# Two linear-attention blocks on one core: the place of A's head selection on VectorE, and which of B's weight buffers holds which sum of pk

## The chip, the core and the metric

The kernel runs on one core of a Trainium2 chip. The core has a matrix engine (TensorE, "PE" in the profile, with its weight loads "PEld"), a vector engine (VectorE, "DVE"), an activation engine (ScalarE, "ACT"), GpSimd ("POOL") and a sync engine (SyncE, "SP") whose queue issues nearly all of the DMAs here. Each engine works through its own instructions in order and waits on semaphores for the others. The metric is the device time of one execution in microseconds; of several runs the median is given.

## The reference

Two blocks A and B with weights of their own read the same x (2048 rows of 640), and a gate mixes their outputs:

```python
qkv = ((x @ wqkv).reshape(B, S, 3, H, Dh)).transpose(2, 0, 3, 1, 4)      # H = 32, Dh = 20
q, k, v = qkv[0], qkv[1], qkv[2]
phi = lambda t: jnp.where(t > 0, t + 1, jnp.exp(t)) + 1e-6
pq, pk = phi(q), phi(k)
kv = jnp.einsum("bhsd,bhse->bhde", pk, v)
z = jnp.einsum("bhsd->bhd", pk)
num = jnp.einsum("bhqd,bhde->bhqe", pq, kv)
den = jnp.einsum("bhqd,bhd->bhq", pq, z)[..., None] + 1e-6
block = (num / den).transpose(0, 2, 1, 3).reshape(B, S, D) @ wo
...
g = sigmoid((x * gate_w).sum(-1, keepdims=True))
return g * block_A + (1 - g) * block_B
```

All tensors are bf16.

## The kernel before

**What is computed.** v is never formed. Because v = x wv, the product of pk and v is (x^T pk)^T wv, so each block first makes G = x^T pk, a 640 x 640 matrix kept transposed in halves in `GT`, and then multiplies by wv and keeps only the diagonal blocks of 20 x 20 per head (`kvt_mm`, `kvt_mask` for B, `kv_a` for A). These blocks times wo give one 640 x 640 matrix M per block (`m_a` for A, `m_unit` and `m_half` for B), and the output is pq M, where pq has been multiplied by gate / den beforehand (`scale`, line 551).

**Order of the work.** Both blocks use the same stages: k (`k_chunk`, line 207) and q (`q_unit`, line 256) with phi on ScalarE and VectorE; then `g_all` (line 665) with G; then wv, wo and the output. A's k and q come first, then A's G; then B's k, with A's small products between them; then B's q and B's G; then the output of both blocks together, by seven products of halves in place of eight (class `Pair`). From line 699 on the order of all engines' instructions is the order in which the code issues them (`tc.manual_schedule`), so the place of a line in the code is its place in its engine's queue.

**G in `g_all`.** The fifth column block of x is done by `g_pass`: 16 row tiles i, two matmuls each (`g_mm`, line 297). The other four column blocks are done by `g_strassen`, seven products of halves (`g_prod`, line 324, 16 matmuls each) in place of eight. Its operands are the halves themselves, four differences of x made once (`SX[1]` to `SX[4]`, by `x_sum`, in block A only) and four sums of pk made for each block (`TK[b][1]` to `TK[b][4]`, by `k_sum`). All of these sums are VectorE's (line 501). The seven products in order: x11 b11, SX[2] TK[2], x12 b21, SX[3] TK[3], SX[1] TK[1], x22 TK[4], SX[4] b22.

**z and the normalisation.** Between the row tiles of `g_pass`, ahead of i = 6, PE sums pk over all rows from TK[3] and TK[4] (`z_rows`); ScalarE and VectorE copy the result (`zr`). Ahead of i = 14 `z_pass` issues five small matmuls (line 402), which bring zr into columns, and a VectorE instruction (line 406) that selects the heads by a mask and writes `zsel`. zsel is the weight operand of the denominators (`rec_pass`, lines 171 and 491 to 496), which come on PE directly behind the last row tile. For block A the VectorE work issued ahead of i = 6 is: the copy of zr, the first x difference `x_sum(1)`, the two gate instructions (line 183), and the second x difference `x_sum(2)`.

**Weight buffers.** wk, wv, wq and wo have one buffer each, which serves A's weight first and B's later. B's wk and wq are loaded while A runs. B's wv and wo come last: while B's q and G are computed, their two buffers (and wk's) hold B's sums of pk. Before: T1 is in wv's buffer, T4 in wk's, T2 and T3 share wo's. A buffer is free for its load when its last reader on PE is done. The loads are issued from SP: `load_wo(1)` in the code behind the fourth product (line 359, issue at line 656), `load_w(1, "v")` behind the fifth (line 369, issue at line 641). Nothing else is on SP's queue between the load of M[0] (line 462) and the stores of the output (line 582).

**Behind G in B.** PE's first matmuls behind the seventh product are `kvt_mm(1, kv, 0)` (line 416), which reads wvB and the low half of GT; then come the first product of the output, `kvt_mm(1, kv, 1)`, another product of the output, and `m_unit` (line 476), the first reader of woB. VectorE has in that place the last two GT adds (line 377), the two masks (line 423) and the first of the sums of M.

Of the kernel before, what the change touches and what calls it, by code (L numbers as in the profile page):

```python
# [8 lines left out]
P = 128  # L9
FP32 = mybir.dt.float32  # L10
BF16 = mybir.dt.bfloat16
# [10 lines left out]
HF = D // 2  # L22
# [11 lines left out]
def kernel(  # L34
# [11 lines left out]
    nc = tc.nc  # L46
# [42 lines left out]
    hc, ic = ST // 2, 2 * P  # L89
# [22 lines left out]
    wk = [None, None]  # L112
# [63 lines left out]
    def gate_pass():  # L176

        pt = ps("lg", 2)
        for h in range(2):
            by_group(pt[:, 1, h * RB:(h + 1) * RB], gwr, xT, h)  # L180
        for b in range(2):
            nc.scalar.activation(out=ge[b][:], in_=pt[:, 1, :], func=ACT.Exp, scale=(-1.0, 1.0)[b])
            nc.vector.tensor_scalar(ge[b][:], ge[b][:], 1.0, 1e30, op0=ALU.add, op1=ALU.min)
# [94 lines left out]
    def g_pass(b, c, slot):  # L278

        pt = ps(f"g{'AB'[b]}", slot)  # L280
        for i in range(ST):
            if i == 6:
                zt, zr = z_rows(b, 0)
                if b == 0:
                    x_sum(1)
                    gate_pass()
                    x_sum(2)
            if i == 14:
                zsel = z_pass(zt, zr)
            for hf in range(2):  # L290
                g_mm(c, i, hf, pt)
        for hf in range(2):
            nc.scalar.copy(out=GT[hf][:, c, :], in_=pt[:, hf, 0:HF])
        return zsel
# [7 lines left out]
    def x_sum(k):  # L302

        x11, x21 = [xn[:, 0:hc, n:n + ic] for n in (0, ic)]
        x12, x22 = [xn[:, hc:ST, n:n + ic] for n in (0, ic)]
        a, b, op = {
            1: (x21, x22, ALU.subtract), 2: (x11, SX[1], ALU.subtract),
            3: (x21, x11, ALU.subtract), 4: (x12, SX[2], ALU.subtract),
        }[k]
        add_rows(SX[k], a, b, op)  # L310
# [18 lines left out]
    def g_strassen(b, norm):  # L329

        x11, x12 = [xn[:, k:k + hc, 0:ic] for k in (0, hc)]
        x22 = xn[:, hc:ST, ic:2 * ic]
        b11 = pk[:, 0:hc, 0:HF]
        b21, b22 = [pk[:, hc:ST, n * HF:(n + 1) * HF] for n in range(2)]
        lo, hi = GT

        def temp(name):
            return work.tile([P, 2, HF], FP32, tag="osb", name=name, bufs=3)

        def add(dst, pt, sb):  # L340
            nc.vector.tensor_tensor(out=dst, in0=pt[:, :, 0:HF], in1=sb[:], op=ALU.add)

        even, odd = ps("gs0", 0), ps("gs1", 1)
        g_prod(even, x11, b11, True)
        p1 = temp("p1")
        nc.scalar.copy(out=p1[:], in_=even[:, :, 0:HF])
        g_prod(odd, SX[2], TK[b][2], True)
        u2 = temp("u2")
        add(u2[:], odd, p1)
        if b == 0:  # L350
            x_sum(3)
        norm()
        g_prod(even, x12, b21, False)
        nc.scalar.copy(out=lo[:, 0:2, :], in_=even[:, :, 0:HF])
        scale(b, 0)
        scale(b, 1)
        g_prod(odd, SX[3], TK[b][3], False)
        if b == 1:
            load_wo(1, nc.sync)
        u3 = temp("u3")  # L360
        add(u3[:], odd, p1)
        if b == 0:
            x_sum(4)
        else:
            scale(b, 2)
        even = ps("gs0", 0)
        g_prod(even, SX[1], TK[b][1], True)
        if b == 1:
            wv[1] = load_w(1, "v", nc.sync)
        add(hi[:, 2:4, :], even, u3)  # L370
        scale(b, 3 if b else 2)
        g_prod(odd, x22, TK[b][4], False)
        add(lo[:, 2:4, :], odd, p1)
        scale(b, 4 if b else 3)
        g_prod(even, SX[4], b22, False)
        for n in range(2):
            nc.vector.tensor_tensor(out=hi[:, n, :], in0=even[:, n, 0:HF], in1=u2[:, n], op=ALU.add)
        if b == 0:
            scale(b, 4)
# [319 lines left out]
    with tc.manual_schedule():  # L699
        k_chunk(0, ST - 2)  # L700
        nc.vector.tensor_copy(out=gwr[:], in_=gcol[:, :, None].to_broadcast([P, DT, H]))
        k_chunk(0, ST - 1)
        k_sum(0, 1)
        q_pass(0, [(m, 1) for m in range(DT)], {0: 2, 1: 3, 2: 4}, (1, 2, 3, 4))
        wq[1] = load_w(1, "q", nc.sync)
        g_all(0)

        turn[0] = 1
        for i in range(ST):
            k_chunk(1, i)  # L710
            if i > 3 and i % 2 == 0:
                m_a(i // 2 - 2)
            if i == 1:
                kv_a()
            if i in (3, 6, 9, 12):
                r0 = (i - 3) // 3 * RB
                p_diff(slice(r0, r0 + RB))
        turn[0] = 2
        TK[1][1], TK[1][4] = [wpool.tile([P, hc, HF], BF16, tag=t, name=n)[:] for t, n in (("wv", "T1"), ("wk", "T4"))]
        t = wpool.tile([P, 2, hc, HF], BF16, tag="wo", name="T23")  # L720
        TK[1][2], TK[1][3] = t[:, 0], t[:, 1]
        k_sum(1, 1)
        q_pass(1, [(m, h) for h in range(2) for m in range(DT)], {0: 2, 2: 3, 4: 4}, (3, 5, 7))
        g_all(1)
        banks.close()
        outer = ctx.enter_context(late_pool("outer"))
        TM[3] = wpool.tile([P, DT, HF], BF16, tag="wk", name="TM3")
        t = wpool.tile([P, 2, DT, HF], BF16, tag="wq", name="TM12")
        TM[1], TM[2] = t[:, 0], t[:, 1]
        part = [slice(n * RB, (n + 1) * RB) for n in range(4)]  # L730
        half = ST // 2
        acc = {k: [bank(outer, f"o{k}{n}") for n in range(2)] for k in "zx"}
        pairs = [Pair(i) for i in range(half)]
        with late_pool("mid") as mid:
            first = bank(mid, "mid0", 2)
            kv = bank(mid, "mid1", 2)
            kvt_mm(1, kv, 0)
            kvt_mask(kv, 0)
            add_rows(TM[0][:], M[0][:, :, HF:D], M[0][:, :, 0:HF], ALU.subtract)
            pairs[0].p1()  # L740
            kvt_mm(1, kv, 1)
            kvt_mask(kv, 1)
            p_sums(part[0], (1, 2))
            pairs[1].p1()
            m_unit(1, 0, "act", first)
            m_unit(1, 1, "act", bank(mid, "mid1", 2))
            m_sums((0, 1), (2, 1))
        with late_pool("single") as single:
            for hf in range(2):
                m_half(1, 2, hf, acc["z"][hf][:, 0:HF])  # L750
                nc.scalar.copy(out=M[1][:, 2, hf * HF:(hf + 1) * HF], in_=acc["z"][hf][:, 0:HF])
            m_sums((2,), (2, 1))
            m_unit(1, 3, "act", bank(single, "s3", 2))
            m_sums((3,), (2, 1))
            pts = [bank(single, f"s4{hf}")[:, 0:HF] for hf in range(2)]
            for hf in range(2):
                m_half(1, 4, hf, pts[hf])
            nc.scalar.copy(out=M[1][:, 4, 0:HF], in_=pts[0])
            nc.vector.tensor_copy(out=M[1][:, 4, HF:D], in_=pts[1])
            m_sums((4,), (2, 1))  # L760
        for p in pairs[0:2]:
            p.p5()
        inner = ctx.enter_context(late_pool("inner"))
        acc |= {k: [bank(inner, f"o{k}{n}") for n in range(2)] for k in "wy"}
        for p in pairs[0:2]:
            p.p2()
        p_sums(part[0], (4,))
        m_sums(range(DT), (3,))
        for p in pairs[0:2]:
            p.p7()  # L770
            p.p6()
            p.c22()
            p.c11()
        pairs[0].p4()
        pairs[0].p3()
        later = {2: (2, (1, 2)), 3: (2, (4,)), 4: (3, (2, 4))}
        for i in range(1, half):
            p, after = pairs[i], pairs[i + 1] if i + 1 < half else None
            if i > 1:
                p.p7()  # L780
                p.p6()
                p.p5()
                p.c22()
            if after is not None:
                after.p1()
            if i == 1:
                p_sums(part[1], (1,))
            q = after if i + 2 < half else p if after is None else None
            if q is not None:
                q.p2()  # L790
                q.c11()
            if i == 1:
                p_sums(part[1], (2,))
            p.p4()
            p.p3()
            if i == 1:
                p_sums(part[1], (4,))
            if i in later:
                p_sums(part[later[i][0]], later[i][1])
            if i == 3:  # L800
                p_sums(part[3], (1,))
# [30 lines left out]
```

## Time and profile before

| | |
|---|---|
| median of the runs | 192.01 us |
| lowest and highest of 3 runs | 191.72 and 192.34 us |
| the profiled execution's own time | 192.37 us |
| its span, first to last instruction | 190.5 us |
| PE busy | 183.7 us (96%), 1460 instructions |
| PEld busy | 124.2 us (65%) |
| DVE busy | 150.3 us (79%), 244 instructions |
| ACT busy | 75.0 us (39%) |
| granted clock of PE, mean | 1.000 |
| block A: `g_pass` to the end of the seventh product | about 49.4 to 73.6 us |
| block B: the same | about 119.9 to 142.4 us |

All times in views of the trace are microseconds from the start of the span. A row of a timeline gives start, duration, engine, line, operation, the tile written and the tiles read, and in brackets the idle time of that engine ahead of it with what ended it. The ends of matmuls are modelled, so neighbouring rows of PE can overlap by a few hundredths. "DMA to landing" is the time from the issue of a transfer to its arrival. The chain of waits is followed back from the last instruction: at each step to the work that released it.

### The profile page before, as it was taken

How to read it: one execution, taken by the hardware profiler on the slowest of the kernel's cores; microseconds unless marked ns; L12 is line 12 of the kernel's file. 1: busy time of each engine (PE TensorE's matmuls, PEld its weight loads, DVE VectorE, ACT ScalarE, POOL GpSimd, SP SyncE). 2: the span in 40 equal slices, each digit the busy share in tenths (PEclk: the TensorE clock that was granted, in tenths of full speed). 3: DMA queues.
4: the chain of work that ended last, by engine and by line, in shares of the span. 5: the costliest groups of instructions: out<-in, count | busy, mean ns of one | idle time of the engine just before them, and what ended most of it. 6: DMA issues, size and time to landing. Idle time of an engine off the chain costs nothing.

```text
span 190.5 us, 3574 instructions
## 1 busy us (share of the span) xinstructions
PE 183.7 (96%) x1460; PEld 124.2 (65%) x1465; DVE 150.3 (79%) x244; ACT 75.0 (39%) x106; POOL 2.8 (1%) x17
## 2 busy tenths in 40 slices
PE   8999999999999999999999999999997999999992
PEld 3666657755667677877765555676766776777771
DVE  1478868899988989798989997746996989787553
ACT  2055455538941501366654677315101611111110
POOL 5000000000000000000000000000000000000000
PEclk9999999999999999999999999999999999999999
DMA  5975559970320000011124000000190002312122
GB/s 181 326 140 92 105 89 372 312 213 3 72 105 0 3 0 0 3 32 54 32 57 172 2 0 0 3 0 3 31 283 30 3 3 101 106 69 72 69 71 71
DMA packets 19802, 15.63 MB, mean 82 GB/s; under 512 B 9546, under 2 KB 19658, under 8 KB 19786
## 3 DMA queue, kind: packets, MB, share of 16 engines
q1 hardware_dynamic: 18922, 14.59, 27.8%
q10 hardware_dynamic: 864, 0.82, 1.3%
q8 instruction: 11, 0.18, 0.4%
q14 instruction: 5, 0.04, 0.1%
HBM read 10.00 MB, written 3.44 MB: 71 GB/s over the span
## 4 chain that ended last, share of the span: by engine, by line
PE 91%; DMA 3%; DVE 3%; issue 1%; ACT 1%; DVEq 0%; ACTq 0%
PE gs L324 14%; PE kA L207 12%; PE kB L207 11%; PE qB L256 11%; PE qA L256 7%; PE ox L562 6%; PE oy L562 5%; PE oz L562 5%; PE qA L267 4%; DMA wvB<-in_B_wqkv_dram 3%; PE ow L562 2%; PE gB L297 2%; PE warm L164 2%; DVE osb L567 1%; PE mid L416 1%; DVE S L501 1%
## 5 line engine op out<-in xcount | busy, mean ns | idle before, releaser
L207 PEld LDWEIGHTS <-xT 128*128 128x128 bf16 x320 | 31.2, 99 | 12.6 <-DVE xT L192 0.2
L200 DVE TENSOR_SCALAR e<-e 128x640 bf16<-128x640 bf16 (+1 forms) x52 | 18.7, 360 | 6.4 <-ACT e L197 5.7
L207 PE MATMUL kA<-wkA,xT 128*128 128x320 bf16 x160 | 23.2, 304 | 0.0
L207 PE MATMUL kB<-wkB,xT 128*128 128x320 bf16 x160 | 23.1, 299 | 0.0
L256 PE MATMUL qB<-xT,wqB 128*128 128x512 bf16 x98 | 21.7, 379 | 0.1
L197 ACT ACTIVATE e<-kB 128x640 bf16<-128x640 f32 x16 | 11.3, 704 | 18.8 <-PE kB L207 17.5
L256 PEld LDWEIGHTS <-wqB 128*128 128x128 bf16 x100 | 11.7, 117 | 9.8 <-issue 0.2
L197 ACT ACTIVATE e<-kA 128x640 bf16<-128x640 f32 x16 | 11.1, 704 | 13.1 <-PE kA L207 13.1
L204 DVE SCALAR_TENSOR_TENSOR pk<-kA,e 128x640 bf16<-128x640 f32 x16 | 13.2, 824 | 1.7
L204 DVE SCALAR_TENSOR_TENSOR pk<-kB,e 128x640 bf16<-128x640 f32 x16 | 13.2, 824 | 1.7
L197 ACT ACTIVATE e<-qA 128x1024 bf16<-128x1024 f32 x10 | 10.2, 1024 | 9.3 <-PE qA L267 5.2
L197 ACT ACTIVATE e<-qB 128x1024 bf16<-128x1024 f32 x10 | 10.2, 1024 | 8.7 <-PE qB L256 8.3
L256 PE MATMUL qA<-xT,wqA 128*128 128x512 bf16 x59 | 13.2, 379 | 0.1
L606 ACT COPY u<-ox 128x320 f32<-128x320 f32 x8 | 3.4, 426 | 21.8 <-PE ox L562 21.8
L324 PEld LDWEIGHTS <-S 128*128 128x128 bf16 x96 | 9.4, 98 | 3.6
L324 PEld LDWEIGHTS <-xn 128*128 128x128 bf16 x96 | 9.1, 98 | 4.0 <-issue 0.4
L256 PEld LDWEIGHTS <-wqA 128*128 128x128 bf16 x60 | 7.0, 117 | 5.8
L590 ACT COPY p1s<-ox 128x320 f32<-128x320 f32 x8 | 3.4, 426 | 18.4 <-PE ox L562 18.4
L562 PEld LDWEIGHTS <-xT 128*128 128x128 bf16 x85 | 8.0, 98 | 3.1 <-DVE xT L501 0.2
L562 PEld LDWEIGHTS <-pqTA 128*128 128x128 bf16 x85 | 7.9, 98 | 2.9 <-issue 0.2
L562 PEld LDWEIGHTS <-pqTB 128*128 128x128 bf16 x80 | 7.8, 98 | 3.0
L324 PE MATMUL gs<-pk,xn 128*128 128x320 bf16 x64 | 9.4, 300 | 0.0
(124 smaller groups left out, 286.2 us busy)
## 6 DMA issues: line engine op xcount, KB each, us to landing
out_dram<-osb SPq DMA_DIRECT2D x14, 160.0 KB, 1.8
xn<-in_A_x_dram SPq DMA_DIRECT2D x3, 640.0 KB, 6.4
wqA<-in_A_wqkv_dram SPq DMA_DIRECT2D x1, 800.0 KB, 6.2
wvA<-in_A_wqkv_dram SPq DMA_DIRECT2D x1, 800.0 KB, 9.9
wkB<-in_B_wqkv_dram SPq DMA_DIRECT2D x1, 800.0 KB, 4.7
wqB<-in_B_wqkv_dram SPq DMA_DIRECT2D x1, 800.0 KB, 4.8
MA<-ma_dram SPq DMA_DIRECT2D x1, 800.0 KB, 4.3
woB<-in_B_wo_dram SPq DMA_DIRECT2D x1, 800.0 KB, 6.1
```

What stands on the lines that cost most here:

```text
L164: nc.tensor.matmul(warm[:, 0, :], lhsT=one_l, rhs=one_r, start=True, stop=True)
L197: nc.scalar.activation(out=e[:], in_=src, func=ACT.Exp)
L200: nc.vector.tensor_scalar(e[:], e[:], 1.0, EPS, op0=ALU.min, op1=ALU.add)
L204: nc.vector.scalar_tensor_tensor(out=dst, in0=src, scalar=1.0 + EPS, in1=e[:], op0=ALU.add, op1=ALU.max)
L207: nc.tensor.matmul(pt[:, hf, 0:HF], lhsT=xT[:, c, i * P:(i + 1) * P], rhs=wk[b][:, c, hf * HF:(hf + 1) * HF], start=(c == 0), stop=(c == D ...
L256: nc.tensor.matmul(pt[:, u, :], lhsT=mixed(wq[b][:, c, :], m), rhs=xT[:, c, n * HB:(n + 1) * HB], start=(c == 0), stop=(c == DT - 1),)
L267: nc.tensor.matmul(pt[:, u, :], lhsT=mixed(wq[b][:, c, :], m + u), rhs=xT[:, c, n * HB:(n + 1) * HB], start=(c == 0), stop=(c == DT - 1),)
L297: nc.tensor.matmul(pt[:, hf, 0:HF], lhsT=xn[:, i, c * P:(c + 1) * P], rhs=pk[:, i, hf * HF:(hf + 1) * HF], start=(i == 0), stop=(i == ST - 1),
L324: nc.tensor.matmul(pt[:, n, 0:HF], lhsT=left[:, i, n * P:(n + 1) * P], rhs=right[:, i, :], start=(first and i == 0), stop=(i == hc - 1), s ...
L562: nc.tensor.matmul(dst, lhsT=left[:, c, r0:r0 + P], rhs=right[:, c, :], start=(first and c == 0), stop=(c == DT - 1), skip_group_check=not ...
L590: nc.scalar.copy(out=self.p1s[:], in_=self.at("x"))
L606: nc.scalar.copy(out=self.u2[:], in_=self.at("x"))
```

## The change

Two edits that don't touch each other.

1. In `g_pass` the call of `z_pass` moves from ahead of i = 14 to ahead of i = 13, for both blocks, and in block A `x_sum(2)` moves behind it.
2. For block B, T2 is put into wv's buffer and T1 joins T3 in wo's. So wv's buffer has its last reader in the second product, and wo's in the fifth; the load of wv moves behind the second product, the load of wo behind the fifth.

```diff
@@ g_pass
                 if b == 0:
                     x_sum(1)
                     gate_pass()
+            if i == 13:
+                zsel = z_pass(zt, zr)
+                if b == 0:
                     x_sum(2)
-            if i == 14:
-                zsel = z_pass(zt, zr)
             for hf in range(2):
                 g_mm(c, i, hf, pt)
@@ g_strassen
         g_prod(odd, SX[2], TK[b][2], True)
+        if b == 1:
+            wv[1] = load_w(1, "v", nc.sync)
         u2 = temp("u2")
         add(u2[:], odd, p1)
...
         g_prod(odd, SX[3], TK[b][3], False)
-        if b == 1:
-            load_wo(1, nc.sync)
         u3 = temp("u3")
         add(u3[:], odd, p1)
...
         g_prod(even, SX[1], TK[b][1], True)
         if b == 1:
-            wv[1] = load_w(1, "v", nc.sync)
+            load_wo(1, nc.sync)
         add(hi[:, 2:4, :], even, u3)
@@ behind B's k
         turn[0] = 2
-        TK[1][1], TK[1][4] = [wpool.tile([P, hc, HF], BF16, tag=t, name=n)[:] for t, n in (("wv", "T1"), ("wk", "T4"))]
-        t = wpool.tile([P, 2, hc, HF], BF16, tag="wo", name="T23")
-        TK[1][2], TK[1][3] = t[:, 0], t[:, 1]
+        TK[1][2], TK[1][4] = [wpool.tile([P, hc, HF], BF16, tag=t, name=n)[:] for t, n in (("wv", "T2"), ("wk", "T4"))]
+        t = wpool.tile([P, 2, hc, HF], BF16, tag="wo", name="T13")
+        TK[1][1], TK[1][3] = t[:, 0], t[:, 1]
         k_sum(1, 1)
```

## The prediction

> **What bounds the kernel now.** I read the page's span and its shares of the chain of waits first, then the chain in order of time, then the timeline around every place where the chain leaves TensorE (PE).
>
> ```profile
> span 190.5 us, 3574 instructions
> ...
> PE 91%; DMA 3%; DVE 3%; issue 1%; ACT 1%; DVEq 0%; ACTq 0%
> ```
>
> PE carries 91% of the chain, so an edit pays only where PE stands still, and then it pays that idle time. The DMA's 3% is one transfer. In the chain, in order of time (start, duration, what):
>
> ```profile
> 138.12 5.93 DMA wvB<-in_B_wqkv_dram
> 144.06 0.04 issue
> 144.10 0.96 PE mid L416 x20
> ```
>
> B's wv weights are sent for at 138.12 and PE starts on them the moment they land. The timeline of PE around that place (start, duration, line, operation; in brackets the idle time ahead and what ended it):
>
> ```profile
> 140.10 2.34 PE L324 MATMUL gs<-pk,MB 128*128 128x320 bf16 x16
> 144.10 0.96 PE L416 MATMUL mid<-GT,wvB 128*80 128x80 bf16 x20 [1.66 <-DMA wvB<-in_B_wqkv_dram]
> ...
> 147.17 1.29 PE L476 MATMUL mid<-woB,KVT 80*32 80x320 bf16 x32
> ```
>
> The seventh product ends at 140.10 + 2.34 = 142.44 and the next matmul starts at 144.10: PE is idle for 1.66 us. The first reader of woB, L476, comes at 147.17. The other place is block A's selection of the heads out of z; VectorE (DVE) and PE there:
>
> ```profile
> 54.61 0.42 DVE L183 TENSOR_SCALAR geB<-geB 128x512 f32<-128x512 f32 x1
> 54.95 1.22 DVE L501 TENSOR_TENSOR S<-xn,S 128x2048 bf16<-128x2048 bf16 x1
> 56.08 0.32 DVE L406 TENSOR_TENSOR zsel<-zA,headE 128x160 bf16<-128x160 f32 x1
> 57.78 0.42 DVE L491 SCALAR_TENSOR_TENSOR d<-denA,geA 128x256 f32<-128x256 f32 x1 [1.38 <-PE denA L171]
> ```
>
> ```profile
> 52.92 2.35 PE L297 MATMUL gA<-pk,xn 128*128 128x320 bf16 x16
> 55.10 0.34 PE L402 MATMUL zA<-I,zr 128*128 128x32 bf16 x5
> 55.29 0.70 PE L297 MATMUL gA<-pk,xn 128*128 128x320 bf16 x4
> 56.45 1.28 PE L171 MATMUL denA<-pqTA,zsel 128*32 128x256 bf16 x40 [0.46 <-DVE zsel L406]
> ```
>
> The 1.22 us of the second x difference (the S row) stand in DVE's queue ahead of zsel, so zsel begins at 56.08 although its matmuls began at 55.10, and PE waits 0.46 us for it.
>
> **Part 1, A's selection ahead of the difference.** Nothing is added or removed; one DVE instruction changes places with another and five small matmuls move one step of i (two matmuls) forward. What the order costs without the difference in the way is seen in block B, where that difference isn't computed:
>
> ```profile
> 124.51 0.34 PE L402 MATMUL zB<-I,zr 128*128 128x32 bf16 x5
> 124.70 0.70 PE L297 MATMUL gB<-pk,xn 128*128 128x320 bf16 x4
> 125.33 1.27 PE L171 MATMUL denB<-pqTB,zsel 128*32 128x256 bf16 x40
> ```
>
> ```profile
> 123.23 0.49 DVE L395 TENSOR_TENSOR zr<-zB,zu 128x320 bf16<-128x320 f32 x1 [0.28 <-ACT zr L394]
> 124.89 0.33 DVE L406 TENSOR_TENSOR zsel<-zB,headE 128x160 bf16<-128x160 f32 x1 [1.16 <-PE zB L402]
> ```
>
> In B denB starts 125.33 - 124.70 = 0.63 after the last four g matmuls start. The same in A gives 55.29 + 0.63 = 55.92 in place of 56.45: 0.53 us earlier. Moving the five matmuls among the g matmuls leaves that moment alone, because PE does the same work before it. Is zsel ready by then? Sixteen g matmuls take 55.10 - 52.92 = 2.18, so one step of i takes 0.27, and zA's matmuls start at about 54.83. B's zsel starts 124.89 - 124.51 = 0.38 behind them, which gives 55.21 in A; DVE is free at 54.61 + 0.42 = 55.03. In B denB starts 0.44 behind zsel, so zsel would release denA at 55.65, 0.27 ahead of PE's need. Bounds: the 0.46 that PE's row calls idle, and 0.53 from B's spacing; I take 0.53, since it runs from start to start.
>
> In B the selection moves a step too. Its matmuls would then start at 124.51 - 0.27 = 124.24; zr, which they read, is done at 123.23 + 0.49 = 123.72. B has no wait there, so it gains nothing, and it loses nothing with 0.5 us in hand.
>
> What is late next in A: the difference itself. It starts when zsel is done, near 55.5, and ends near 56.7. Behind it on DVE is d (L491), which waits for denA and had 1.38 us of idle time; it would come at 57.78 - 0.53 = 57.25, so 0.5 us of that cover are left. If the cover were gone, each microsecond would delay d and the two reciprocals behind it. The reader of the difference is the second product on PE:
>
> ```profile
> L324 PEld LDWEIGHTS <-S x96: 97/98/98, 59.7 to 137.7; 128*128 128x128 bf16 x96
> ```
>
> It loads its weights at 59.7 - 0.53 = 59.2, 2.5 us behind the end of the difference. Cost nothing, hidden by the first product.
>
> **Part 2, B's buffers and loads.** The four k sums keep their number and order on DVE; T1 and T2 change places. The two loads keep their sizes; wv is issued three products earlier, behind the second, and wo one product later, behind the fifth, where wv stood. Each waits on SP's queue, with nothing between them and nothing behind but the output stores, which come after the products anyway.
>
> ```profile
> 135.95 0.33 SPq L656 DMA_DIRECT2D woB<-in_B_wo_dram  x1
> 138.12 0.39 SPq L641 DMA_DIRECT2D wvB<-in_B_wqkv_dram  x1
> ```
>
> The landing times (last column, us) of whole weights of 800 KB, first two by themselves, then the two that overlap:
>
> ```profile
> wqB<-in_B_wqkv_dram SPq DMA_DIRECT2D x1, 800.0 KB, 4.8
> MA<-ma_dram SPq DMA_DIRECT2D x1, 800.0 KB, 4.3
> woB<-in_B_wo_dram SPq DMA_DIRECT2D x1, 800.0 KB, 6.1
> wvB<-in_B_wqkv_dram SPq DMA_DIRECT2D x1, 800.0 KB, 5.9
> ```
>
> In today's times, wv goes out after the second product. Three products of 16 matmuls each lie between it and the end of the fifth at 138.12; a product takes about (142.44 - 138.1) / 2 = 2.17, so wv is issued by 138.12 - 3 x 2.17 = 131.6 and lands by 131.6 + 5.9 = 137.5, almost five microseconds ahead of 142.44. The 1.66 us of idle time have no other cause: GT's low half is finished by the add behind the sixth product, while the seventh runs, and the PSUM banks of the new pool were emptied far earlier. Gain 1.66. Since B's g matmuls at 124.70 + 0.70 = 125.40 overrun their successor's start by 0.07, PE may restart 0.07 sooner than the modelled end: upper bound 1.73.
>
> wo goes out at 138.12 and lands at 144.22 with its own 6.1, though no other load runs beside it now; its reader L476 would come at 147.17 - 1.66 = 145.51. Slack 1.29 us, or 2.6 to 3.1 with the 4.8 or 4.3 of loads that ran alone. Both ends leave it hidden; I take 6.1, its own row. The Trainium skill's SBUF — State Buffer (Door 1: The DMA port swizzle) states that only the ports that a transfer's partitions reach carry it, at about 27 GB/s each, beside a fixed 2 us or so: wo's 80 partitions put 8 rows of 10,240 bytes on the fullest port, which makes an estimate of 5.0 us against 3.9 for wv's 128 partitions. That speaks against putting wo last, and the order of the rows agrees with it (6.1 against 4.3 and 4.8, though 6.1 was not alone); the sum would be the same by either.
>
> Two checks on costs of nothing. Do loads slow PE, now that wv runs beside products? And can T1 enter wo's buffer in time?
>
> ```profile
> L324 PE MATMUL gs<-T,S x48: 299/299/299, 128.7 to 137.8; 128*128 128x320 bf16 x48
> ...
> L501 DVE TENSOR_TENSOR T<-pk x2: 1481/1481/1481, 100.4 to 108.2; 128x2560 bf16<-128x2560 bf16 x2
> ```
>
> ```profile
> L455 PE MATMUL mA<-woA,KVA x12: 297/300/302, 81.7 to 96.8; 120*120 120x320 bf16 x8, 80*80 80x320 bf16 x4
> ```
>
> The products' matmuls last 299 ns whether or not woB is in flight. T1 is written first of the sums, at 100.4; the last reader of woA starts at 96.8 and lasts 0.3, so the buffer has been free for 3.3 us. Without that cover DVE would stall in order, with the phi work of B's q units behind it.
>
> What is late next at the restart is DVE:
>
> ```profile
> 142.47 0.89 DVE L377 TENSOR_TENSOR GT<-gs,u 128x320 bf16<-128x320 f32 x2 [0.22 <-PE gs L324]
> 145.09 0.49 DVE L423 TENSOR_TENSOR KVT<-mid,maskE 80x320 bf16<-80x320 f32 x1 [1.73 <-PE mid L416]
> 145.50 0.98 DVE L501 TENSOR_TENSOR TM<-MA 128x1600 bf16<-128x1600 bf16 x1
> ```
>
> The mask would be wanted at 145.09 - 1.66 = 143.43; the last GT adds end at 142.47 + 0.89 = 143.36. The 1.73 of idle time shrink to 0.07, but stay above zero. Should DVE slip there, the most I see is one mask's 0.49 handed on to L476 through the second mask: lower bound 1.66 - 0.49 = 1.17.
>
> **The sum.** 0.53 + 1.66 = 2.19 us. The profiled execution took 192.37 us, its span 190.5, so 1.87 lie outside the span and stay: span 188.3, that execution 190.18. It was 0.36 above the median of the runs, 192.01; against the median the forecast is 192.01 - 2.19 = 189.82.
>
> **The rivals.**
> (a) DVE becomes the gate at the restart. For it: the 0.07. Against it: zsel's and d's idle times show DVE waiting for PE before it, and nothing is added to it. 192.01 - 0.53 - 1.17 = 190.31.
> (b) A's half is swallowed downstream: some wait between 57 and 98 that is set by DVE or ScalarE. Against it: DVE waits 1.38 for denA, so its whole queue moves with denA, and the loads that B's k and q need have landed by then. 192.01 - 1.66 = 190.35.
> (c) The change doesn't do what it says: the wv load still leaves near 138, because its buffer is given back by something later than the second product. Against it: SP is in order and nothing waits ahead of it. Only 0.53 is left: 191.48.
> (d) Slower: the wait moves to wo. From 2.19 less, L476 wants wo at 144.98, and it is issued at 138.12 - 0.53 = 137.59, so it may take 7.39. Beyond that PE stalls at L476, and beyond 7.39 + 2.19 = 9.58 the kernel is slower than before. Such landings are seen for A's wo:
>
> ```profile
> DMA to landing us min/median/max: 8.8/9.3/10.3
> ```
>
> At 10.3 the price is 10.3 - 7.39 = 2.91, the time 192.01 - 2.19 + 2.91 = 192.73. Against it: those four transfers left together with A's x and wv, while woB runs alone.
>
> **How the numbers follow.** The forecast itself 75 in 100, (a) 12, (b) 6, (c) 3, (d) 3, something I don't see 1, counted as slower. A measurement of this kernel can tell 0.3%, 0.58 us, from no change: the forecast, (a) and (b) are faster, 0.93; (c) is within it, 0.03; slower 0.04. The range: the gains run from 0.46 + 1.17 = 1.63 to 0.53 + 1.73 = 2.26, so 189.75 to 190.38 on the median; the runs of before lie from 0.29 below it to 0.33 above (191.72 to 192.34), and three runs show less than the whole spread, so I add 0.45 below and 0.5 above: 189.3 to 190.9. That holds (a) and (b).
>
> **What would show it.** Right: in A zsel's row stands ahead of the second S row, denA's row has no idle time, and d follows its S row with about 0.5 idle; the wv issue stands near 131, the wo issue near 137.6; L416 starts within 0.1 of the seventh product's end, near 141.9, with no DMA in the chain of waits; L476 has no wait for woB, near 145.0; the tail to the end is the old one shifted by 2.2. Wrong: PE waiting for woB at L476 (d), for DVE at L476 or L416 (a), a new wait of PE between 57 and 98 (b), or a wv issue past 136 (c).

## The result and the profile after

| | before | after |
|---|---|---|
| median of 6 runs each | 192.10 us | 190.03 us |
| lowest and highest | 191.69 and 192.56 | 189.17 and 191.13 |
| the profiled execution's own time | 192.37 | 189.94 |
| its span | 190.5 | 188.1 |

The ratio after to before is 0.9892, with a 95% interval from 0.9863 to 0.992: of 192.1 us that is 2.1 us less (1.5 to 2.6). The forecast was 189.8, in a range of 189.3 to 190.9.

Block A in the profile after, first VectorE's timeline, then TensorE's (line numbers are one higher behind the first edit):

```profile
54.77 0.42 DVE L183 TENSOR_SCALAR geB<-geB 128x512 f32<-128x512 f32 x1
55.44 0.32 DVE L407 TENSOR_TENSOR zsel<-zA,headE 128x160 bf16<-128x160 f32 x1 [0.25 <-PE zA L403]
55.68 1.22 DVE L502 TENSOR_TENSOR S<-xn,S 128x2048 bf16<-128x2048 bf16 x1
57.41 0.42 DVE L492 SCALAR_TENSOR_TENSOR d<-denA,geA 128x256 f32<-128x256 f32 x1 [0.52 <-PE denA L171]
```

```profile
54.99 0.34 PE L403 MATMUL zA<-I,zr 128*128 128x32 bf16 x5
55.18 0.97 PE L298 MATMUL gA<-pk,xn 128*128 128x320 bf16 x6
56.08 1.28 PE L171 MATMUL denA<-pqTA,zsel 128*32 128x256 bf16 x40
```

The selection now stands ahead of the S row, denA's row has lost its 0.46 us of idle time, and d's idle time has shrunk from 1.38 to 0.52: the difference took up cover that VectorE had.

Behind B's seventh product, TensorE and then VectorE:

```profile
139.72 2.34 PE L325 MATMUL gs<-pk,MB 128*128 128x320 bf16 x16
141.90 0.93 PE L417 MATMUL mid<-GT,wvB 128*80 128x80 bf16 x20
142.66 0.85 PE L563 MATMUL ox<-MA,pqTA 128*128 128x320 bf16 x5
143.44 0.92 PE L417 MATMUL mid<-GT,wvB 128*80 128x80 bf16 x20
```

```profile
142.10 0.89 DVE L378 TENSOR_TENSOR GT<-gs,u 128x320 bf16<-128x320 f32 x2 [0.21 <-PE gs L325]
142.91 0.48 DVE L424 TENSOR_TENSOR KVT<-mid,maskE 80x320 bf16<-80x320 f32 x1
143.30 0.98 DVE L502 TENSOR_TENSOR TM<-MA 128x1600 bf16<-128x1600 bf16 x1
```

TensorE goes on without a wait; the mask has no idle time ahead of it any more, where it had 1.73. The two loads leave SP's queue here:

```profile
130.72 0.39 SPq L642 DMA_DIRECT2D wvB<-in_B_wqkv_dram  x1
137.75 0.34 SPq L657 DMA_DIRECT2D woB<-in_B_wo_dram  x1
```

wv leaves 7.4 us earlier than before (138.12), and each load lands 5.7 us behind its issue. The chain of waits holds no DMA in this stretch.

The two executions are best compared by stretches that begin and end at a start of the same TensorE group. The view of windows for before and for after; the columns are the window, its length, busy time of each engine with its instructions, the granted clock, DMA share and GB/s:

```profile
49.45:56.45 7.00, 6.54 (x94) 4.55 (x92) 6.68 (x11) 4.36 (x9) 0.00 (x0) 1.00 0.40 119
56.45:125.33 68.88, 68.77 (x513) 46.01 (x515) 58.80 (x83) 32.40 (x43) 0.00 (x0) 1.00 0.08 25
125.33:144.10 18.77, 17.11 (x161) 11.98 (x161) 14.30 (x15) 4.06 (x6) 0.00 (x0) 1.00 0.35 88
144.10:147.17 3.07, 3.07 (x51) 2.46 (x51) 1.96 (x4) 0.43 (x1) 0.00 (x0) 1.00 0.00 0
147.17:190.50 43.33, 39.77 (x361) 29.23 (x360) 31.87 (x70) 9.27 (x21) 0.00 (x0) 1.00 0.19 62
```

```profile
49.61:56.08 6.47, 6.47 (x94) 4.55 (x92) 5.96 (x11) 3.93 (x7) 0.00 (x0) 1.00 0.42 129
56.08:124.96 68.88, 68.77 (x514) 46.00 (x516) 59.62 (x84) 32.80 (x43) 0.00 (x0) 1.00 0.08 25
124.96:141.90 16.94, 16.94 (x162) 12.09 (x162) 13.42 (x13) 4.06 (x6) 0.00 (x0) 1.00 0.34 91
141.90:144.97 3.07, 3.07 (x53) 2.42 (x50) 2.75 (x6) 0.43 (x1) 0.00 (x0) 1.00 0.17 35
144.97:188.10 43.13, 39.78 (x361) 29.23 (x360) 31.88 (x70) 9.26 (x21) 0.00 (x0) 1.00 0.19 62
```

Stretch 1 runs from A's first g matmul to A's denominators, stretch 2 from there to B's denominators, stretch 3 to the first matmul on wvB, stretch 4 to the first on woB, stretch 5 to the end. Stretch 1 lost 0.53 us, stretch 3 lost 1.83, stretches 2 and 4 nothing. The start came 0.16 later (49.61 against 49.45), and stretch 5 is 0.20 shorter, all of it behind TensorE's last matmul, which ends 3.56 us ahead of the end before and 3.36 after. Together 0.16 - 0.53 - 1.83 - 0.20 = -2.40, which is 188.1 - 190.5. So the edits are worth 2.36 us in these two profiles. The rest is not theirs: in the twelve runs below stretch 5 lies between 43.09 and 43.28, whatever the edit.

### The profile page after: what moved, and what is told of

The parts are those of the page before. It is cut to its first block, busy times and chain, and to the rows that moved or that the text cites. A ratio compares the mean times of both kernels' runs of the same rounds, so it can differ in the third digit from the quotient of the medians.

```text
span 188.1 us, 3574 instructions
## 1 busy us (share of the span) xinstructions
PE 182.7 (97%) x1460; PEld 123.5 (66%) x1465; DVE 150.3 (80%) x244; ACT 75.0 (40%) x106; POOL 2.8 (2%) x17
## 4 chain that ended last, share of the span: by engine, by line
PE 93%; DMA 3%; DVE 1%; ACTq 0%; issue 0%; ACT 0%; DVEq 0%
PE gs L325 16%; PE kB L207 12%; PE qB L256 11%; PE kA L207 11%; PE qA L256 7%; PE ox L563 6%; PE oy L563 5%; PE oz L563 5%; PE qA L267 5%; DMA xn<-in_A_x_dram 3%; PE ow L563 3%; PE gB L298 2%; PE gA L298 2%; DVE osb L568 1%; PE mA L456 1%; PE mid L417 1%
## 5 line engine op out<-in xcount | busy, mean ns | idle before, releaser
L207 PE MATMUL kA<-wkA,xT 128*128 128x320 bf16 x160 | 22.6, 299 | 0.1
L197 ACT ACTIVATE e<-kB 128x640 bf16<-128x640 f32 x16 | 11.3, 704 | 18.8 <-PE kB L207 17.5
```

What stands on the lines that cost most here:

```text
L197: nc.scalar.activation(out=e[:], in_=src, func=ACT.Exp)
L207: nc.tensor.matmul(pt[:, hf, 0:HF], lhsT=xT[:, c, i * P:(i + 1) * P], rhs=wk[b][:, c, hf * HF:(hf + 1) * HF], start=(c == 0), stop=(c == D ...
```

## The experiments

The stretches of every run, each from its own timeline of TensorE (the start of the named group less the start of the one before); "start" is where A's first g matmul begins.

| run | start | 1 | 2 | 3 | 4 | time, us |
|---|---|---|---|---|---|---|
| before | 49.45 | 7.00 | 68.88 | 18.77 | 3.07 | 192.10 |
| after | 49.61 | 6.47 | 68.88 | 16.94 | 3.07 | 190.03 |
| e1_head_only | 49.26 | 6.48 | 68.88 | 18.65 | 3.07 | 191.42 (11 runs) |
| e2_buffers_only | 49.38 | 7.00 | 68.88 | 16.94 | 3.07 | 190.29 (6 runs) |
| e3_order_alone | 48.62 | 6.48 | 68.88 | 18.55 | 3.06 | 190.65 (one) |
| e4_step_alone | 50.06 | 7.00 | 68.88 | 18.50 | 3.07 | 192.57 (one) |
| e5_wo_sixth | 48.74 | 6.48 | 68.87 | 16.94 | 3.07 | 189.16 (one) |
| e6_wo_seventh | 49.91 | 6.48 | 68.87 | 16.94 | 3.07 | 190.13 (7 runs) |
| e7_wv_then_wo | 49.94 | 7.01 | 68.88 | 18.08 | 3.06 | 192.04 (one) |
| e8_tm_ahead | 49.73 | 6.48 | 68.87 | 16.94 | 3.97 | 191.09 (one) |
| e9_old_lines | 49.00 | 6.48 | 68.88 | 20.94 | 4.53 | 195.09 (4 runs) |
| e10_wo_held | 50.61 | 6.48 | 68.88 | 16.93 | 3.72 | 191.78 (one) |
| e11_own_bank | 49.22 | 6.47 | 68.88 | 16.94 | 2.98 | 189.72 (one) |
| e12_bank_only | 49.49 | 6.48 | 68.87 | 16.94 | 2.98 | 189.72 (4 runs) |

The times come from four sessions. The median of before beside them was 192.10 for after, 192.28 for e1 to e4, 192.18 for e5 to e8 and 192.55 for e9 to e12, so small differences between rows of the last column mean nothing.

**The two parts by themselves.** e1_head_only is before with the first edit alone:

```diff
+            if i == 13:
+                zsel = z_pass(zt, zr)
+                if b == 0:
                     x_sum(2)
-            if i == 14:
-                zsel = z_pass(zt, zr)
```

> Part 1 alone. In the profiles of before and after, the stretch from the first g matmul of A to the first denominator matmul is 56.45 - 49.45 = 7.00 us and 56.08 - 49.61 = 6.47, and from the first denominator matmul of B to the first matmul on wvB 144.10 - 125.33 = 18.77 and 141.90 - 124.96 = 16.94. Theory (two gains, each in its own place, that add): first stretch 6.47, second 18.77, time 0.53 us under before. Rival (A's half is swallowed later): first stretch 6.47, but the 68.88 us from A's denominators to B's grow by up to 0.5 and the time stays.

Stretch 1 is 6.48, stretch 2 is unchanged, and the ratio to before is 0.9963 (0.9939 to 0.9987), that is 0.7 us less (0.2 to 1.2). A's half isn't swallowed: 69 us of work follow it at the same length to 0.01. Stretch 3 is 18.65, 0.12 under the expected 18.77, although nothing was changed there: wv landed in 5.8 us, not 5.9. In e3 and e4, which keep before's buffers too, it landed in 5.7 and stretch 3 is 18.55 and 18.50. Against the 16.94 of after, wv's wait in the kernel before is therefore 1.56 to 1.83 us, depending on that landing.

e2_buffers_only is after with the first edit undone:

```diff
+                    x_sum(2)
-            if i == 13:
+            if i == 14:
                 zsel = z_pass(zt, zr)
-                if b == 0:
-                    x_sum(2)
```

> Part 2 alone. Theory: first stretch 7.00 us, second 16.94, so 1.83 us under before, and no DMA wait of TensorE behind the seventh product. Rival (the loads' gain depends on A's half, or part of it is lost at the masks): second stretch between 16.94 and 18.77 - 1.17 = 17.60.

Stretch 3 is 16.94, the ratio 0.9884 (0.9864 to 0.9904), 2.2 us less (1.8 to 2.6). The halves add by stretches: 0.52 and 1.83 by themselves, 0.53 and 1.83 together. The times of e2 and after can't be told apart, though they differ by the 0.53; the last section shows the scatter that hides it.

**What in the first edit does it.** e3_order_alone moves the difference behind the selection and leaves the five matmuls at i = 14; e4_step_alone moves the matmuls to i = 13 and leaves the difference ahead.

```diff
e3
-                    x_sum(2)
             if i == 14:
                 zsel = z_pass(zt, zr)
+                if b == 0:
+                    x_sum(2)
e4
-            if i == 14:
+            if i == 13:
                 zsel = z_pass(zt, zr)
```

> Before, with the second x difference behind the selection, but the selection's matmuls still ahead of row tile 14. Theory (the 1.22 us of the difference on VectorE are the whole cost): the selection starts about 0.4 behind its matmuls, so the first stretch is 6.47 to 6.6 us. Rival (the step from 14 to 13 carries the gain): first stretch 6.8 to 7.0.

> Before, with the selection's matmuls ahead of row tile 13, but the difference still ahead of the selection on VectorE. Theory: nothing gained, first stretch 7.00 us, because VectorE reaches the selection when the difference is done. Rival (the step carries the gain): 6.7 or less.

TensorE in e3 and then in e4:

```profile
54.28 0.34 PE L403 MATMUL zA<-I,zr 128*128 128x32 bf16 x5
54.46 0.70 PE L298 MATMUL gA<-pk,xn 128*128 128x320 bf16 x4
55.10 1.17 PE L171 MATMUL denA<-pqTA,zsel 128*32 128x256 bf16 x36
```

```profile
55.45 0.34 PE L402 MATMUL zA<-I,zr 128*128 128x32 bf16 x5
55.63 0.97 PE L297 MATMUL gA<-pk,xn 128*128 128x320 bf16 x6
57.06 1.17 PE L171 MATMUL denA<-pqTA,zsel 128*32 128x256 bf16 x36 [0.46 <-DVE zsel L406]
```

The order on VectorE carries the whole gain. The step forward gains nothing without it, and at most 0.01 us with it: it is slack and no more.

**When a load leaves.** e5_wo_sixth and e6_wo_seventh were meant to send wo later, by moving its line:

```diff
         g_prod(even, SX[1], TK[b][1], True)
-        if b == 1:
-            load_wo(1, nc.sync)
         add(hi[:, 2:4, :], even, u3)
...
         g_prod(odd, x22, TK[b][4], False)
+        if b == 1:
+            load_wo(1, nc.sync)
```

That is e5; in e6 the two lines stand behind the seventh product:

```diff
         g_prod(even, SX[4], b22, False)
+        if b == 1:
+            load_wo(1, nc.sync)
```

> After, with the load of wo behind the sixth product in place of the fifth, 2.17 us later. In after it is issued at 137.75, lands in 5.7 us at 143.45 and is read at 144.97: 1.5 us in hand. Theory (it lands in 5.7 us wherever it is issued): issue 139.9, landing 145.6, so TensorE waits 0.6 to 0.7 us at the first matmul on woB, and the stretch from the first matmul on wvB to the first on woB grows from 3.07 to about 3.7 us. Rival (a load by itself lands in 4.3 to 5.0 us, and the 5.7 is chance): 3.07 to 3.1 us.

> After, with the load of wo behind the seventh product, 4.3 us later than in after. Theory: issue near 142.1, landing near 147.8, TensorE waits about 2.8 us at the first matmul on woB, and the time is 190.0 + 2.8 = 192.8 us, slower than before by about 0.7: the slower case of the prediction, made on purpose. Rival (a load by itself lands in 4.3 to 5.0 us): a wait of 1.4 to 2.1 us and a time of 191.4 to 192.1.

Both expectations fell, and not by the rival's reason. SP's queue in e6, and the sixth product there:

```profile
131.02 0.39 SPq L642 DMA_DIRECT2D wvB<-in_B_wqkv_dram  x1
138.05 0.34 SPq L657 DMA_DIRECT2D woB<-in_B_wo_dram  x1
```

```profile
137.85 2.34 PE L325 MATMUL gs<-T,xn 128*128 128x320 bf16 x16
140.03 2.34 PE L325 MATMUL gs<-pk,MB 128*128 128x320 bf16 x16
```

The wo load leaves at 138.05, as the sixth product begins, though its line stands behind the seventh. SP has nothing else to do there, so its load waits for nothing but the last reader of the buffer, T1's, in the fifth product. The line by itself is worth nothing; 190.13 us and the stretches are those of after.

e10_wo_held really holds the buffer one product longer, by giving T4 (read by the sixth product) to it:

```diff
-        TK[1][2], TK[1][4] = [wpool.tile([P, hc, HF], BF16, tag=t, name=n)[:] for t, n in (("wv", "T2"), ("wk", "T4"))]
-        t = wpool.tile([P, 2, hc, HF], BF16, tag="wo", name="T13")
-        TK[1][1], TK[1][3] = t[:, 0], t[:, 1]
+        TK[1][2], TK[1][1] = [wpool.tile([P, hc, HF], BF16, tag=t, name=n)[:] for t, n in (("wv", "T2"), ("wk", "T1"))]
+        t = wpool.tile([P, 2, hc, HF], BF16, tag="wo", name="T43")
+        TK[1][4], TK[1][3] = t[:, 0], t[:, 1]
```

(The wo line stands where e5 has it.)

> After, with wo's buffer really held one product longer: T4, which the sixth product reads, shares wo's buffer with T3, and T1 goes to wk's. Theory: wo is issued at the end of the sixth product, 2.17 us later than in after, 1.98 ahead of the first matmul on wvB; it lands 5.7 us later, 3.72 behind that matmul, and its reader wanted it 3.07 behind: TensorE waits 0.6 to 0.8 us at the first matmul on woB and that stretch is 3.65 to 3.85 us. Rival (a load by itself lands in 4.3 to 5.0 us): 3.07 to 3.1 us.

```profile
140.92 0.34 SPq L657 DMA_DIRECT2D woB<-in_B_wo_dram  x1
```

```profile
142.90 0.93 PE L417 MATMUL mid<-GT,wvB 128*80 128x80 bf16 x20
143.66 0.85 PE L563 MATMUL ox<-MA,pqTA 128*128 128x320 bf16 x5
144.44 0.93 PE L417 MATMUL mid<-GT,wvB 128*80 128x80 bf16 x20
145.19 0.85 PE L563 MATMUL ox<-MA,pqTA 128*128 128x320 bf16 x5
146.62 0.61 PE L477 MATMUL mid<-woB,KVT 80*32 80x320 bf16 x12 [0.58 <-DMA woB<-in_B_wo_dram]
```

wo lands 5.7 us behind its issue again, at 146.62, and stretch 4 is 3.72: inside the expectation. This is the prediction's slower case (d) at its first step. From after's wo load, 1.5 us are in hand (137.75 + 5.7 = 143.45 against 144.97), and what is taken beyond them is paid in full: 2.17 later cost 0.65.

**Queue order.** e9_old_lines keeps after's buffers and puts before's lines back: the wo line behind the fourth product, the wv line behind the fifth.

```diff
-        if b == 1:
-            wv[1] = load_w(1, "v", nc.sync)
         u2 = temp("u2")
...
         g_prod(odd, SX[3], TK[b][3], False)
+        if b == 1:
+            load_wo(1, nc.sync)
...
         g_prod(even, SX[1], TK[b][1], True)
         if b == 1:
-            load_wo(1, nc.sync)
+            wv[1] = load_w(1, "v", nc.sync)
```

> After's buffers with before's lines: the load of wo stands in the code behind the fourth product, the load of wv behind the fifth. In the two runs that moved the wo line behind the sixth and the seventh product, its issue stayed at the end of the fifth. Theory (a load leaves when its buffer's last reader is done and the loads ahead of it on SP's queue have left): wo, first in the queue, waits for the fifth product, and wv, whose buffer is free since the second, stands behind it: wo issued near 138.1 in before's times, wv 0.4 behind it, the stretch from B's denominators to the first matmul on wvB 18.8 to 19.5 us, a time of 192.0 to 193.0, no better than before and perhaps slower. Rival (the buffer alone decides): 16.94 us and 190.0.

```profile
137.14 0.33 SPq L657 DMA_DIRECT2D woB<-in_B_wo_dram  x1
137.53 0.51 SPq L642 DMA_DIRECT2D wvB<-in_B_wqkv_dram  x1
```

wv's buffer is free from the second product on, but its load stands behind wo's on SP's queue and leaves 0.39 us behind it. The theory holds, its size was too small: wv's load now runs beside wo's from its start and takes 7.7 us to land, so TensorE waits 3.84 us and stretch 3 is 20.94, above the expected 18.8 to 19.5:

```profile
145.30 1.56 PE L417 MATMUL mid<-GT,wvB 128*80 128x80 bf16 x20 [3.84 <-DMA wvB<-in_B_wqkv_dram]
```

Stretch 4 grew too, by 1.46 us, without any wait in it. The windows of TensorE's clock in e9 (the eighth entry, ahead of the DMA share):

```profile
141.00:145.00 4.00, 0.46 (x4) 0.10 (x1) 1.17 (x3) 0.00 (x0) 0.00 (x0) 1.00 0.93 252
145.00:147.00 2.00, 1.70 (x22) 1.58 (x23) 0.10 (x1) 0.00 (x0) 0.00 (x0) 0.57 0.00 0
147.00:149.00 2.00, 2.00 (x24) 1.58 (x23) 1.29 (x2) 0.42 (x1) 0.00 (x0) 0.58 0.00 0
149.00:151.00 2.00, 2.00 (x47) 1.54 (x48) 1.70 (x3) 0.79 (x2) 0.00 (x0) 1.00 0.04 8
```

The kernel is slower than before: ratio 1.0144 (1.0097 to 1.0192), with the very buffers of after. So the second edit needs both its halves: the buffer that comes free early, and the wv load ahead of wo's on the queue.

e7_wv_then_wo asks the reverse: before's buffers, both loads behind the fifth product, wv first.

```diff
         g_prod(odd, SX[3], TK[b][3], False)
-        if b == 1:
-            load_wo(1, nc.sync)
...
         if b == 1:
             wv[1] = load_w(1, "v", nc.sync)
+            load_wo(1, nc.sync)
```

> Before, with its buffers as they were, but both loads behind the fifth product, wv ahead of wo. It tells the place of the wv load from its sharing the DMA engines with wo. Theory (the place decides, sharing costs little): wv is issued near 138.1 in before's times and lands in 5.7 to 5.9 us; the wait ahead of the first matmul on wvB stays 1.4 to 1.7 us, the second stretch 18.5 to 18.8. Rival (wv was late because wo was in flight ahead of it): it lands in 4.3 to 4.8 us, the wait is 0.2 to 0.6, the second stretch 17.1 to 17.6, and wo takes up a wait of its own behind it.

wv leaves at 138.62 and lands in 5.2 us; stretch 3 is 18.08, between what the two expected. That is 0.69 of the 1.83 us. It is the faster landing, 5.2 us for 5.9. But wv landed in 5.6 to 6.1 us in the other runs where its load had the engines to itself, and in 5.7 to 5.9 behind wo's in before, e1, e3 and e4. So these runs show no cost of wo's load being in flight ahead of it by 2.17 us, and how much of the 0.69 is chance one run can't say.

The other 1.14 us belong to the place: with before's buffers wv's is free only at the end of the fifth product, and neither order of the two loads (wo's first in before, wv's first in e7) gained them. The profile names VectorE, not the DMA, as what ended this wait:

```profile
143.91 0.96 PE L415 MATMUL mid<-GT,wvB 128*80 128x80 bf16 x20 [0.97 <-DVE GT L376]
```

These adds write the high half of GT, which this product doesn't read, and in after the same product starts at 141.90, ahead of the adds at 142.10. So the wait is for wv, which landed near 138.62 + 5.2 = 143.82.

wo landed 7.9 us behind its issue, at 146.96, where its reader starts at 146.97: no slack was left.

**VectorE at the restart.** e8_tm_ahead puts the 0.98 us of TM0 ahead of the first mask:

```diff
             kvt_mm(1, kv, 0)
-            kvt_mask(kv, 0)
             add_rows(TM[0][:], M[0][:, :, HF:D], M[0][:, :, 0:HF], ALU.subtract)
+            kvt_mask(kv, 0)
```

> After, with the 0.98 us of the first sum of M (TM0) ahead of the first mask on VectorE instead of behind it. It asks whether VectorE is the gate at the restart, where its last idle time is gone. Theory (the masks have slack as a pair, since the second one waits for TensorE anyway): the first mask starts about 1 us later, the second within 0.1 of where it was, and the stretch from the first matmul on wvB to the first on woB stays 3.07 to 3.15 us. Rival (case a: VectorE gates): the second mask is handed the delay, the stretch grows to 3.5 us or more.

```profile
142.02 0.93 PE L417 MATMUL mid<-GT,wvB 128*80 128x80 bf16 x20
142.78 0.85 PE L563 MATMUL ox<-MA,pqTA 128*128 128x320 bf16 x5
144.46 0.92 PE L417 MATMUL mid<-GT,wvB 128*80 128x80 bf16 x20 [0.83 <-DVE KVT L424]
```

Stretch 4 grew by 0.90 us: the theory fell, and VectorE does gate here. But the delay isn't handed on as the prediction had it, through the second mask to the first reader of woB. TensorE itself stops at the second product with wv, until the first mask is done. That product writes the other half of the PSUM tile `kv` that the mask still reads. e11_own_bank is e8 with that product in another tile, and e12_bank_only is after with the same edit:

```diff
-            kvt_mm(1, kv, 1)
-            kvt_mask(kv, 1)
+            kvt_mm(1, first, 1)
+            kvt_mask(first, 1)
```

> The run with TM0 ahead of the first mask made TensorE wait 0.83 us at the second product with wv for the first mask, and the stretch from the first matmul on wvB to the first on woB was 145.99 - 142.02 = 3.97. Here, in the same kernel, the second product with wv writes into the other PSUM tile (first, bank 1) in place of the first one's tile. Theory (the wait is for the shared PSUM tile, which the first mask still reads): the wait at the second product goes, and the stretch is 3.0 to 3.3 us. Rival (VectorE is late for the masks whatever the tile): the delay moves to the first matmul on woB, and the stretch is 3.5 us or more.

> After, with nothing but the second product with wv in the other PSUM tile. Theory: in after that product starts 0.05 us behind the end of the first mask, so the tile costs it at most 0.1 us: stretch 2.97 to 3.07 us, time within 0.1 of after's, which a comparison with before can't tell from after. Rival (the tile costs after more than that): 2.9 us or less.

In e11 the stretch is 2.98, just under the expected 3.0 to 3.3, with VectorE as late as in e8. Its timeline:

```profile
141.71 0.89 DVE L378 TENSOR_TENSOR GT<-gs,u 128x320 bf16<-128x320 f32 x2 [0.22 <-PE gs L325]
142.52 0.98 DVE L502 TENSOR_TENSOR TM<-MA 128x1600 bf16<-128x1600 bf16 x1
143.42 0.99 DVE L424 TENSOR_TENSOR KVT<-mid,maskE 80x320 bf16<-80x320 f32 x2
```

Both masks now run back to back from 143.42 to 144.41, and TensorE's first matmul on woB starts at 144.49. So the wait was the shared tile's. Without it VectorE's microsecond of lateness is hidden, with 0.08 us between the masks' end and that matmul. In e12 the stretch is 2.98 too: after pays 0.09 us for the tile, against the 0.1 that was allowed (before has the same 3.07 as after, so the edits didn't add this). Its median is 189.72 (189.48 to 190.02) and its ratio 0.986 (0.9811 to 0.9908): better than after by the stretch, not to be told from it by time.

## Why the prediction was right, point by point

- **A's selection, 0.53 us: right, and for its reason.** The selection ahead of the difference gives 0.53, e3 shows that the order carries it, and stretch 2 shows that nothing behind gives it back (rival (b)). The estimate that denA would start 0.63 us behind the last four g matmuls is e3's 55.10 - 54.46 = 0.64. The ready moment of zsel was missed by 0.07 us: it starts 55.44 - 54.99 = 0.45 behind its matmuls, not 0.38, inside the 0.27 of cover.
- **The difference behind the selection: free, as said.** d had 0.52 us of idle time left, the prediction 0.5.
- **wv's wait, 1.66 us: right in mechanism, too small.** It was worth 1.83 in the profile that the 1.66 was read from, above even the upper bound of 1.73. The idle time in a TensorE row counts from the modelled end of the last matmul. The seventh product's row is 2.34 long, but its successor, when ready, starts 141.90 - 139.72 = 2.18 behind its start. The A term was taken from start to start and held to 0.01; the same for this term (144.10 - 140.10 - 2.18) would have been 1.82. The other profiles with before's buffers show the same gap: rows with 1.55, 1.44 and 1.39 us of idle time (e1, e3, e4) against 1.71, 1.61 and 1.56 in stretch 3. They also show what the prediction left out: the term moves with the landing of one load, by more than this error.
- **wo's slack: right.** The prediction gave 1.29 us with the landing of 6.1, it was 1.5 with 5.7, and e10 shows the price beyond it. The other end, 4.3 to 4.8 us as for the loads that ran alone, was not reached: by itself wo landed in 5.6 to 5.9 us in eight profiles.
- **The rule weighed there.** The Trainium skill's SBUF — State Buffer (Door 1: The DMA port swizzle, and for the fixed 2 us the section on the setup-cost knee behind it) was worked out to 5.0 us for wo's 80 partitions against 3.9 for wv's 128. Here both landed in 5.7, each with the engines to itself, so neither estimate was met and the difference isn't seen in the landing; the measurement decides. It is seen in the rate. The view of DMA in after gives GB/s in 40 slices of 0.5 us from 128 us on:

```profile
GB/s 0 0 0 0 0 0 0 76 77 189 315 384 381 205 26 18 0 0 0 0 0 72 148 151 387 266 215 225 164 10 0 0 0 0 0 33 0 0 0 0
```

In it wv's load holds 315 to 384 GB/s in its main part; wo's falls from 387 to 266, 215 and 225, as a load with fewer ports would. wv's loses that lead in a tail of two slices at 26 and 18 GB/s. What makes the tail is open.
- **Loads beside products: free, as said.** The three products in wv's shadow and those in wo's keep their length; stretch 3 has 16.94 us busy of 16.94.
- **Rival (a), VectorE as the gate: not taken, but nearer than its price said.** Its idle time went to zero at the mask, and e8 shows that a microsecond of lateness costs 0.90, not one mask's 0.49, by way of the shared tile.
- **Rival (c):** the prediction put the risk on the buffer's release. e9 shows that the queue's order would have done it too, and worse.
- **The sum.** 0.53 + 1.66 = 2.19 against 2.36 in the stretches and 2.07 (1.5 to 2.6) in the medians. The medians can't tell 2.19 from 2.36, so that 189.8 came within 0.3 us of 190.03 is in part luck; the stretches carry the account.

## What to carry to other kernels

A load into a reused buffer leaves when that buffer's last reader is done and the loads ahead of it on its queue have left; where its line stands changes only the second of these. So give the temporary that dies first the buffer of the weight that is wanted first, put that load first on the queue, and then count the next transfer's slack. Measure gains from start to start of the same groups, not by idle times that hang on a modelled end, and look at what else shares a tile with the engine that has just lost its slack.

## What the hardware showed that was not expected

**An idle TensorE lost half its clock at a length between 1.66 and 3.84 us.** Before stood still for 1.66 us and kept a granted clock of 1.00. e9 stood still for 3.84. From its restart at 145.30 to 148.50 the granted clock was 0.50, and 0.81 in the half microsecond behind; the two windows above, which hold some full speed at their ends, average 0.57 and 0.58. Its first group with wv took 1.56 us, not 0.93, and stretch 4 grew from 3.07 to 4.53. All four runs of e9 have a mean clock of 0.991. The Trainium skill's TensorE: Matmul & The Clock Gate (HAM oscillation — how this bites in real kernels) warns of gaps of more than about 3.4 us, after which the clock falls to half; the two lengths here lie on either side of that figure and agree with it, and two lengths don't show more. In e9 the wait cost 1.46 us more than its own length.

**Most of the scatter of the profiled executions comes from their first nine microseconds.** A's first g matmul began between 48.62 and 50.61 us, a spread of 1.99 us and nearly the whole gain, although nothing was changed ahead of it. Stretch 5, behind all the edits, spreads by 0.24 us only (43.09 to 43.33). The fourth transpose of x, near the beginning, moves with it: it began at 7.46 and 9.45 in the runs at those two ends (e3 and e10), and 41.16 us lie between it and the first g matmul in both. In e10 it waited for x to land:

```profile
9.45 0.45 PE L188 MATMUL xt<-ident,xn 128*128 128x128 bf16 x5 [1.05 <-DMA xn<-in_A_x_dram]
```

So e3's single time of 190.65 us, 1.6 below the median of the runs of before beside it (192.28), says little about e3, whose stretches are worth 0.52 and 0.22. Why x lands at different times, and whether the executions without a profile scatter for the same reason, is open.
